# A token table in DRAM whose neighbouring places move 1152 bytes apart

## The chip, the cores and the metric

The kernel runs on one core of a Trainium2 chip. The metric is the device time of one execution in microseconds (us), lower is better. The engines named below are PE (TensorE, matrix products and transposes), DVE (VectorE), ACT (ScalarE), POOL (GpSimd) and SP (SyncE, which here only issues DMAs). All DMAs of the core, whether SP or POOL issues them, run on the same 16 DMA engines.

## The reference

Block-causal attention over 8 batches and 8 heads (576 tokens, head dimension 64, blocks of 64), then a mixture of 8 experts in which every token goes to the one expert with the largest router logit.

```
scores = q @ k.T / sqrt(64); masked to key block <= query block; softmax; out = attn @ v
x = out as (4608, 512)
logits = normalized(x) @ normalized(expert_emb).T / tau
e = argmax(logits); g = softmax(logits)[e]
out[e == i] = g * (relu(x[e == i] @ w1[i]) @ w2[i])      # w1: 512 x 1024, w2: 1024 x 512
```

## The kernel before

**Attention** works on 32 pairs of heads, four pairs to a batch. A step of the main loop computes the scores of one pair, the products with the values of the pair before, the row maxima of the next pair and the operands of the one after. The order of these parts within a step is written out by hand in strings of letters (`PLANS`): s, v, f, m, p, l for the parts of attention, and **r** for one piece of "other work", which is the router of the batch that has just ended. Each engine runs its instructions in the order in which they are written.

A row maximum goes a long way round: DVE reduces (line 338), PE transposes, ACT copies the result to `nmT` (line 345), and SP issues two small DMAs that put it as a row into `qx` (line 347). The score products of the next pair (lines 367 and 368, PE) cannot begin without it.

**The router** of a batch (`route`) finds the expert of each of the 576 tokens, its gate, and its rank within the expert. From these, `places` works out the place of the token: first place of the expert plus rank. The batch's rows of x go to DRAM (`xbuf`, lines 472 and 473), and then five indirect DMAs, issued by POOL (line 575), write 1 + token number into the place of each token in a DRAM table. Each of the five takes the 128 rows of one query tile and writes single numbers of 4 bytes, each to the address that its index gives: 576 in all, since 64 of the 640 rows stand for no token and are dropped. Seven of the eight batches do this, so 35 such DMAs run. The table has 36864 places, 36 x 128 for each of 8 experts, and place i stands at byte 4 i; ranks of an expert that follow each other are 4 bytes apart.

**The table is read twice**, both times by SP. After the seventh batch, `early_rows` reads the first 256 places (`et`, line 600), from which POOL gathers the first tokens of expert 0 (`ex`). SP takes its work in order, and the read waits for all table writes; behind it in SP's order stand the two `qx<-nmT` DMAs of the last pair. Later the whole table is read as 288 rows of 512 bytes (`tsb`, line 1014), and a product with one-hot columns (line 799) spreads the rows over the expert slots.

**The experts** follow: PE runs about 1700 products of 128 x 128 with 512 columns in split precision, nearly without a gap.

PE's sums of the softmax (lines 408 to 413) use partial sums `pS`, which POOL adds up (line 358, four additions for each head).

Of the kernel before, what the change touches and what calls it, by code (L numbers as in the profile page):

```python
# [8 lines left out]
F32 = mybir.dt.float32  # L9
F32R = mybir.dt.float32r  # L10
BF16 = mybir.dt.bfloat16
# [6 lines left out]
# of a pair of heads: the order of the parts of its scores (s), of the products with the values of  # L18
# the pair before (v) and its ends (f), of the maxima of the next pair (m), of the operands of the
# one after (p), the loads (l), and parts of the router's preparation (k) and of other work (r)  # L20
# [14 lines left out]
def kernel(  # L35
# [12 lines left out]
    nc = tc.nc  # L48
# [5 lines left out]
    NJ = (S - 64) // P + 1          # query tiles: 64 rows, then 128 each; key tiles: 128 each, then 64  # L54
    SP = NJ * P
    NTILE = B * NJ
    RW = DM + 8                     # row of x, its gate, padding
    NSLOT = NT // P + E - 1
    NFL = 5
    EARLY = 2                       # slots of the first expert that hold tokens of all batches but the last  # L60
# [7 lines left out]
    xbuf = dram.tile([NT + 1, RW], F32, name="xbuf")     # row 0: zeros; row t + 1: x of token t, its gate  # L68
    # 1 + token of each place of each expert, RE rows of places for each; 0 where empty
# [7 lines left out]
    ident = const.tile([P, P], F32, name="ident")  # L77
    make_identity(nc, ident)
    triS = const.tile([P, P], BF16, name="triS")        # triS[p, t] = p < t
# [9 lines left out]
    upto = const.tile([P, E, E], F32, name="upto")      # upto[e, f] = f <= e  # L89
# [8 lines left out]

    erev = iota("erev", [P, NJ, E], [[0, NJ], [-1, E]], E)              # E - e
    ebase = iota("ebase", [P, NJ, E], [[0, NJ], [RE * P, E]])           # first place of an expert  # L100
    tokf = iota("tokf", [P, B, NJ], [[S, B], [P, NJ]], 1 - 64, 1)       # 1 + token of row p of tile (b, j)
    gi = iota("gi", [P, NSLOT], [[1, NSLOT]])
    pio = iota("pio", [P, P], [[1, P]])
    # of each row of the table: its expert, as a one-hot, and its rank in the expert's rows
# [8 lines left out]
    drop = const.tile([P, NJ], F32, name="drop")        # large for the rows of tile 0 that stand for nothing  # L113
# [3 lines left out]
    # of each expert: its early slots; what lacks of their places is spread over the partitions  # L117
# [9 lines left out]
    acc = const.tile([P, E], F32, name="acc")           # one-hots summed over tiles  # L127
# [11 lines left out]
    CW = 1024                       # columns of a piece of the weights  # L139
# [14 lines left out]
    Q0 = 64                         # tokens stand 64 columns in, so that tile j is columns 128 j ..  # L154
    SPLIT = 5 * 64                  # queries whose sums stand in the first part
# [25 lines left out]
    NR = 6                          # tiles of q and k as they are loaded  # L181
# [11 lines left out]
    def load_v(n):  # L193
        # tiles of 128 rows, then 64
        b, h0, a = n // NP, 2 * (n % NP), vo[n % NV]
        for hh in range(2):
            nc.sync.dma_start(a[:, 0:NJ - 1, hh, :], v[b, h0 + hh, 0:S - 64, :].rearrange("(j p) d -> p j d", p=P))
        nc.sync.dma_start(a[0:64, NJ - 1, :, :], v[b, h0:h0 + 2, S - 64:S, :].rearrange("h p d -> p h d"))

    # what follows runs in the order it is written in, engine by engine  # L200
# [8 lines left out]
    # operands of the scores, split in two parts: qb = [qh; ql], qx = [qh; mask, -max],  # L209
    # ka = [kh; kh], kx = [kl; mask, ones]; scores^T = ka^T qb + kx^T qx  # L210
# [4 lines left out]
    # qh of both heads, block by block of 64, as a block diagonal; kh of both heads  # L215
    NB = S // 64
    KX = 64 + NJ + 1                # rows of qx and kx
# [34 lines left out]
    # of a pair of heads: identity, and the router's columns of each head  # L252
# [27 lines left out]
    def prep(n):  # L280
        """q and k of a pair of heads: transposed and split."""
# [46 lines left out]
    def maxes(n):  # L328
        """-max of each row of scores, into a row of qx."""
# [20 lines left out]
    # columns of P^T: key tile t holds queries 128 t .. S  # L350
# [3 lines left out]
    def add(ps, t, pT):  # L354
        """ps += key tile t of P^T; ps begins as the part of tile 0 past the first 128 queries."""
        r, w = (P if t < NJ - 1 else 64), S - P * t
        o = ps[0:r, P * (t - 1):S - P]
        nc.gpsimd.tensor_tensor(o, pT[0:r, P:S] if t == 1 else o, pT[0:r, off[t]:off[t] + w], op=ALU.add)  # L358

    def scores(n, pTs):  # L360
        """P^T = exp(scale (scores^T - max)) of a pair of heads, a key tile at a time."""
# [27 lines left out]
    def values(n, pTs):  # L389
        """out^T of a pair of heads side by side, and the sums of its rows."""  # L390
# [13 lines left out]
        # rows 0 and 32: queries up to SPLIT of either head; rows 64 and 96: the SPLIT last ones  # L404
# [15 lines left out]
    JB = 3                      # query tiles in the first of two banks  # L420

    def finish(n, xrow, rin, lgh, ssp):
        """x of a pair of heads, and its part of the router's products."""
# [9 lines left out]
        # sums of the rows of each query tile: of tile 0; of 1 and 2 and, from the same columns, 3 and 4  # L433
# [30 lines left out]
        if n >= NPAIR - NP:         # the last batch: its sums of squares pair by pair  # L464
# [17 lines left out]
    def route(b, xrow, lgh, ssp):  # L482
        """expert, gate and row of xbuf of the tokens of a batch."""
# [12 lines left out]
        # first of the largest  # L496
# [8 lines left out]
        # rank within the expert  # L505
# [24 lines left out]
        if b == B - 2:  # L530
            # the first expert's next rank: past its early slots
# [12 lines left out]
        # gate: of the scaled logits, less their largest  # L544
# [10 lines left out]
        if b < B - 1:  # L555
            rowj = yield from places(t2, ohb)
# [32 lines left out]
    def indices(eng, rows, outs, tk, none):  # L589
        """rows of xbuf and of the output of a table of tokens."""  # L590
# [6 lines left out]
    def early_rows():  # L597
        et = rt.tile([P, EARLY], F32, name="et")
        none = rt.tile([P, EARLY], F32, name="enone")
        nc.sync.dma_start(et, table[0:EARLY * P, :].rearrange("(p j) o -> p (j o)", j=EARLY))  # L600
# [15 lines left out]
    def places(t, ohb):  # L616
        """place of each token: its rank and what its expert's places start at."""
# [4 lines left out]
        nc.vector.tensor_reduce(row, t, axis=AX.X, op=ALU.add)  # L622
        yield
# [33 lines left out]
    def post(n):  # L657
        """what is left of a pair of heads after its products with the values."""
# [30 lines left out]
    # a step: a part of the scores of a pair of heads, of the values of the pair before, and of what  # L689
    # else is due: maxima of the next pair, operands of the one after, ends of the one before  # L690
# [25 lines left out]
    # weights of expert e lie, split in two, in half e % 2 of the rings; those of the next  # L716
    # expert are split in while this one's slots run, and the raw ones of the one after loaded
# [34 lines left out]
    def counts():  # L752
        """slots of each expert: those up to its last, those before its first."""
# [16 lines left out]
        # first place of an expert's table, its early slots before the others  # L770
# [3 lines left out]
    def slot_tokens():  # L774
        """rows of xbuf and of the output, of each place of each slot."""
# [445 lines left out]
```

## Time and profile before

| | us |
|---|---|
| three runs, median (lowest, highest) | 978.39 (975.14, 980.23) |
| span of the profiled execution | 972.5 |
| PE busy in it | 914.2 (94%) |
| DVE, ACT, POOL busy | 533.6, 456.4, 335.6 |

The span runs from the first to the last instruction of the program; what lies around it in an execution is not in the profile, whose own time is told by the span alone. The median of the runs is 5.9 us above the span. The attention takes the first 490 us, the experts the rest. The page's busy share is an average over both; what a change in the attention is worth has to be read from the waits there.

### The profile page before, as it was taken

The numbers are of one execution on the slowest core, as the hardware profiler recorded it, in microseconds if no ns is written. First come the engines' busy times: TensorE is split into PE (matmuls) and PEld (weight loads), VectorE is DVE, ScalarE is ACT, GpSimd is POOL, SyncE is SP. The second block draws the span as 40 slices with busy tenths as digits, with TensorE's granted clock in tenths as the row PEclk, the third lists the DMA queues.
The fourth block names the chain that finished last, engine by engine and source line by source line (L and its number), as shares of the span: only waits on it lengthen the run. The fifth ranks groups of instructions, "written<-read, shape, count | busy, mean of one in ns | idle before, by whom it ended". The sixth has DMA issues, their size and how long they took to land. (4 is left out here: it accounts for less than half of the span.)

```text
span 972.5 us, 19818 instructions
## 1 busy us (share of the span) xinstructions
PE 914.2 (94%) x5426; PEld 714.0 (73%) x5426; DVE 533.6 (55%) x1269; ACT 456.4 (47%) x923; POOL 335.6 (35%) x436
## 2 busy tenths in 40 slices
PE   5999899698998979898699999999999999999996
PEld 4677677476676757676477888888888888888885
DVE  8678677386686857777188544644343222442221
ACT  4567657275575746656366343444343222342221
POOL 5444646246364553636443111111111111111111
PEclk8899999798998999989699999999999999999999
DMA  8858679669685848767347634544444111111101
GB/s 159 174 120 165 157 147 166 93 132 151 135 183 117 168 102 161 168 138 171 115 136 239 217 132 131 188 156 132 132 131 133 45 45 46 34 47 43 44 28 54
DMA packets 155406, 122.47 MB, mean 126 GB/s; under 512 B 122233, under 2 KB 123689, under 8 KB 155260
## 3 DMA queue, kind: packets, MB, share of 16 engines
q1 hardware_dynamic: 147532, 100.14, 45.4%
q0 software_dynamic: 7728, 20.70, 6.7%
q8 instruction: 52, 0.85, 0.4%
q14 instruction: 94, 0.77, 0.3%
HBM read 72.98 MB, written 19.71 MB: 95 GB/s over the span
## 5 line engine op out<-in xcount | busy, mean ns | idle before, releaser
L377 ACT ACTIVATE pT<-pss 128x448 f32<-128x448 f32 (+1 forms) x254 | 112.8, 451 | 150.9 <-PE pss L368 112.5
L338 DVE TENSOR_REDUCE nmx<-psm 128x1 f32<-128x320 f32 x315 | 135.2, 453 | 67.7 <-PE psm L336 57.5
L961 POOL DMA_INDIRECT out_dram<-y,outi x36 | 36.1, 1002 | 356.7 <-DVE y L960 336.6
L367 PE MATMUL pss<-qb,ka 128*128 128x448 f32 (+1 forms) x382 | 130.9, 353 | 16.5 <-ACT pT L377 16.5
L358 POOL TENSOR_TENSOR pS<-pT 128x448 f32<-128x448 f32 x64 | 73.0, 1141 | 175.1 <-ACT pT L377 175.0
L368 PE MATMUL pss<-qx,kx 70*128 70x448 f32 (+1 forms) x382 | 113.5, 321 | 19.6 <-DMA qx<-nmT 19.6
L358 POOL TENSOR_TENSOR pS<-pS,pT 128x320 f32<-128x320 f32 (+2 forms) x192 | 114.1, 594 | 31.6 <-ACT pT L377 10.0
L921 PE MATMUL py<-ring_h,hh 128*128 (+1 forms) x288 | 116.4, 404 | 0.4 <-ACT hh L954 0.4
L399 PE MATMUL psb<-pT,vo 128*64 128x64 f32 (+5 forms) x768 | 114.9, 416 | 1.1 <-DVE lgh L458 1.1
L921 PE MATMUL py<-ring_h,hl 128*128 (+1 forms) x288 | 113.7, 395 | 1.7 <-DVE hl L955 1.7
L921 PE MATMUL py<-ring_l,hh 128*128 (+1 forms) x288 | 112.7, 391 | 0.0
L921 PE MATMUL ph<-ring_h,xh 128*128 x280 | 112.2, 401 | 0.0
L921 PE MATMUL ph<-ring_h,xl 128*128 x280 | 109.7, 392 | 0.0
L921 PE MATMUL ph<-ring_l,xh 128*128 x280 | 109.3, 390 | 0.0
L367 PEld LDWEIGHTS pss<-qb,ka 128*128 128x128 f32 x382 | 76.5, 200 | 38.2 <-ACT pT L377 20.0
L913 DVE TENSOR_TENSOR xl<-px,xh 128x512 fp32r<-128x512 f32 x35 | 24.2, 690 | 145.4 <-ACTq L888 119.0
L954 ACT CAST hh<-px 128x512 fp32r<-128x512 f32 x72 | 38.7, 589 | 135.1 <-PE px L952 129.8
L939 ACT ACTIVATE h<-ph 128x512 f32<-128x512 f32 x70 | 41.8, 597 | 126.0 <-ACTq L888 73.5
L336 PE MATMUL psm<-kd,qd 128*128 128x320 f32 x315 | 91.7, 355 | 3.8 <-ACT kd L316 1.9
L368 PEld LDWEIGHTS pss<-qx,kx 70*128 70x128 f32 x382 | 77.4, 203 | 21.4 <-issue 10.4
L741 DVE TENSOR_TENSOR ring_l<-raw,ring_h 128x1024 f32 (+1 forms) x64 | 77.3, 1248 | 25.4 <-ACT ring_h L737 25.3
L336 PEld LDWEIGHTS psm<-kd,qd 128*128 128x128 f32 x315 | 56.7, 200 | 41.0 <-ACT pT L384 14.6
(237 smaller groups left out, 1619.7 us busy)
## 6 DMA issues: line engine op xcount, KB each, us to landing
raw<-in_moe_w_dram SPq DMA_DIRECT2D x64, 512.0 KB
ka<-kd SPq DMA_DIRECT2D x128, 144.0 KB
qn<-in_q_dram SPq DMA_DIRECT2D x64, 144.0 KB
kn<-in_k_dram SPq DMA_DIRECT2D x64, 144.0 KB
qx<-qb SPq DMA_DIRECT2D x32, 288.0 KB
vo<-in_v_dram SPq DMA_DIRECT2D x64, 128.0 KB
xbuf<-xrow SPq DMA_DIRECT2D x7, 1040.0 KB
qx<-nmT SPq DMA_DIRECT2D x64, 2.2 KB
```

Of the source, the lines that this page charges most:

```text
L336: nc.tensor.matmul(mx[:, 0:max(e - a, 256)], qd[d][:, j, :, :], kd[d][:, a:a + max(e - a, 256)], start=True, stop=True)
L338: nc.vector.tensor_reduce(m[:, j + u:j + u + 1], mx[:, 0:e - a], axis=AX.X, op=ALU.max, negate=True)
L358: nc.gpsimd.tensor_tensor(o, pT[0:r, P:S] if t == 1 else o, pT[0:r, off[t]:off[t] + w], op=ALU.add)
L367: nc.tensor.matmul(o, ka[i][:, hh, ts], qb[i][:, hh, c0:c1], start=True, stop=False)
L368: nc.tensor.matmul(o, kx[i][0:KX, hh, ts], qx[i][0:KX, hh, c0:c1], start=False, stop=True)
L377: nc.scalar.activation(pT[:, o:o + c1 - c0], st[:, 0:c1 - c0], AF.Exp, scale=scale)
L399: nc.tensor.matmul(ob[hh * D:(hh + 1) * D, c0:c1], a[0:r, t, hh, :], pTs[hh][0][0:r, o:o + c1 - c0], start=(t == 0), stop=(c0 == 448 or t ...
L741: return eng.tensor_tensor(piece(ring_l, to, c, half), raw[i][:, c * CW:(c + 1) * CW], piece(ring_h, to, c, half).bitcast(F32), op=ALU.sub ...
L921: m = nc.tensor.matmul(out, a[:, c, :], w, start=(c == 0 and w is wh and a is sh), stop=(c == nk - 1 and a is sl_))
L939: nc.scalar.activation(h[:, f:f + 512], ph, AF.Relu)
L954: nc.scalar.copy(hh[:, f:f + 4, :], ptv)
L961: nc.gpsimd.indirect_dma_start(out=out, out_offset=bass.IndirectOffsetOnAxis(ap=to, axis=0), in_=y, in_offset=None, bounds_check=NT - 1, o ...
```

## The change

A place keeps its number, but stands elsewhere. Place i = 128 r + p, which stood at byte 4 i, now stands at entry 288 p + r, that is at byte 1152 p + 4 r. Ranks of an expert that follow each other are therefore 1152 bytes apart, except where p goes from 127 back to 0. `table_rows` takes the place of `places` for the seven batches that write the table. The readers follow: `et` takes the first two entries of each of 128 rows, and the whole table is read as 128 rows of 1152 bytes (`tbt`), transposed on PE in three pieces and copied by DVE into a tile that holds `tsb`.

```
-            rowj = yield from places(t2, ohb)
+            rowj = yield from table_rows(t2, ohb)
...
-        nc.sync.dma_start(et, table[0:EARLY * P, :].rearrange("(p j) o -> p (j o)", j=EARLY))
+        nc.sync.dma_start(et, table.rearrange("(p r) o -> p (r o)", p=P)[:, 0:EARLY])
...
+    def table_rows(t, ohb):
+        row = sm.tile([P, NJ], F32, name="row")
+        rowt = sm.tile([P, NJ], I32, name="rowt")
+        rowj = sm.tile([P, NJ], I32, name="rowj")
+        nc.vector.tensor_tensor(t, t, ohb, op=ALU.mult)
+        yield
+        nc.vector.tensor_reduce(rowj, t, axis=AX.X, op=ALU.max)
+        yield
+        nc.vector.tensor_scalar(rowt, rowj, P - 1, None, op0=ALU.bitwise_and)
+        yield
+        nc.vector.tensor_scalar(row, rowt, float(E * RE) - 1.0 / P, None, op0=ALU.mult)
+        yield
+        nc.vector.scalar_tensor_tensor(row, rowj, 1.0 / P, row, op0=ALU.mult, op1=ALU.add)
+        yield
+        nc.vector.tensor_tensor(rowj, row, drop, op=ALU.add)
+        yield
+        return rowj
...
-    tsb = st.tile([RC, NCH, P], F32, name="tsb")
-    nc.sync.dma_start(tsb, table.rearrange("(c p t) o -> p c (t o)", p=RC, t=P))
+    tbt = st.tile([P, NCH * RC], F32, name="tbt")
+    nc.sync.dma_start(tbt, table.rearrange("(p r) o -> p (r o)", p=P))
...
+    tsb = sets["xg"][0][0:RC, 0:NCH * P].rearrange("r (c t) -> r c t", t=P)
+    tps = ps_m.tile([P, 512], F32, name="psm")
+    for c in range(NCH):
+        nc.tensor.transpose(tps[0:RC, c * P:(c + 1) * P], tbt[:, c * RC:(c + 1) * RC], ident)
+    nc.vector.tensor_copy(tsb, tps[0:RC, 0:NCH * P].rearrange("r (c t) -> r c t", t=P))
     ch = chain()
```

The new function has three more pieces (`yield`) than the old one, so what follows it in `route` comes three r's later in the plan. In six of the seven batches POOL's order stays as it was. In the seventh it does not. POOL there before, from the router's power (`ss`) on; `pS` are the softmax sums and `table<-tokf,rowj` the table writes:

```order
L553 TENSOR_TENSOR ss<-ss,half 128x5
L358 TENSOR_TENSOR pS<-pS,pT 128x320
L358 TENSOR_TENSOR pS<-pS,pT 128x192
L358 TENSOR_TENSOR pS<-pS,pT 64x64
L575 DMA table<-tokf,rowj 36864x1 x5
L358 TENSOR_TENSOR pS<-pT 128x448
L358 TENSOR_TENSOR pS<-pS,pT 128x320
```

and after:

```order
L554 TENSOR_TENSOR ss<-ss,half 128x5
L359 TENSOR_TENSOR pS<-pS,pT 128x320
L359 TENSOR_TENSOR pS<-pS,pT 128x192
L359 TENSOR_TENSOR pS<-pS,pT 64x64
L576 DMA table<-tokf,rowj 36864x1 x3
L359 TENSOR_TENSOR pS<-pT 128x448
L359 TENSOR_TENSOR pS<-pS,pT 128x320
L359 TENSOR_TENSOR pS<-pS,pT 128x192
L359 TENSOR_TENSOR pS<-pS,pT 64x64
L576 DMA table<-tokf,rowj 36864x1 x2
```

Four additions now stand ahead of the last two table writes. DVE in the same batch, from the product with the one-hots (`t`, `ohb`) to the gate, before:

```order
L620 TENSOR_TENSOR t_5707<-t_5707,ohb 128x40
L622 TENSOR_REDUCE row<-t_5707 128x5
L286 TENSOR_TENSOR kx_183<-pst,kd_188 64x576
L624 TENSOR_TENSOR rowj<-row,drop 128x5
L557 TENSOR_SCALAR ss<-ss 128x5
```

and after:

```order
L634 TENSOR_TENSOR t_5731<-t_5731,ohb 128x40
L636 TENSOR_REDUCE rowj<-t_5731 128x5
L287 TENSOR_TENSOR kx_183<-pst,kd_188 64x576
L638 TENSOR_SCALAR rowt<-rowj 128x5
L640 TENSOR_SCALAR row<-rowt 128x5
L642 SCALAR_TENSOR_TENSOR row<-rowj,row 128x5
L644 TENSOR_TENSOR rowj<-row,drop 128x5
L339 TENSOR_REDUCE nmx_190<-psm 128x1
L558 TENSOR_SCALAR ss<-ss 128x5
```

Three small operations come in ahead of `rowj`, which the table writes wait for. On PE the three transposes stand between the last softmax sums and the first expert products, after:

```order
L410 MATMUL psb<-pS,ones 32x320
L414 MATMUL psb<-pS,ones 32x192 x2
L1072 MATMUL psm<-ident,tbt 96x128 x3
L941 MATMUL pss<-ring_h_6165,xh_6178 128x512
L941 MATMUL pss<-ring_l_6166,xh_6178 128x512
```

Before, the products of line 921 (now 941) followed the sums of line 413 (now 414) directly. DVE's copy of the result stands between two pieces of the weights' split and the last pair's `rin`. SP's order is the same, with `tbt` in the place of `tsb`.

## Rows read from the trace of the kernel before

**Rows 1.** Page: span; then engine, busy us, share, instructions.
```profile
span 972.5 us, 19818 instructions
PE 914.2 (94%) x5426; PEld 714.0 (73%) x5426; DVE 533.6 (55%) x1269; ACT 456.4 (47%) x923; POOL 335.6 (35%) x436
```
**Rows 2.** Windows: length; busy PE, PEld, DVE, ACT, POOL; clock; DMA; GB/s. Experts.
```profile
600.00:700.00 100.00, 100.00 (x493) 83.38 (x492) 47.72 (x64) 42.11 (x62) 16.40 (x17) 1.00 0.50 167
```
**Rows 3.** Tile table, its writes (ns min/median/max); SP's waits (us, times, longest).
```profile
L575 POOL DMA_INDIRECT table<-tokf,rowj x35: 966/972/1126, 110.2 to 456.5; - x35
...
SPq L600 <- DMA table<-tokf,rowj: 15.2, 1, 15.2
```
**Rows 4.** Timeline, seventh batch: start, us, instruction [idle before <- what ended it].
```profile
451.37 1.03 POOL L575 DMA_INDIRECT table<-tokf,rowj  x1 [0.45 <-DVE gs L565]
...
456.52 0.97 POOL L575 DMA_INDIRECT table<-tokf,rowj  x1 [0.30 <-issue]
457.50 1.15 POOL L358 TENSOR_TENSOR pS<-pT 128x448 f32<-128x448 f32 x1
458.74 1.92 POOL L358 TENSOR_TENSOR pS<-pS,pT 128x320 f32<-128x320 f32 x3
...
468.15 0.33 SPq L600 DMA_DIRECT2D et<-table  x1
468.58 1.58 SPq L347 DMA_DIRECT2D qx<-nmT  x2
...
470.47 0.61 PE L368 MATMUL pss<-qx,kx 70*128 70x288 f32 x1 [6.62 <-DMA qx<-nmT]
```
**Rows 5.** Windows, as in Rows 2, after the seventh batch's table writes.
```profile
456.00:458.00 2.00, 2.00 (x17) 1.96 (x17) 0.45 (x2) 0.17 (x1) 1.69 (x3) 1.00 0.71 34
...
464.00:466.00 2.00, 0.00 (x0) 0.00 (x0) 0.00 (x0) 0.09 (x1) 0.15 (x1) 1.00 0.00 0
```
**Rows 6.** Windows after table writes of the second and fourth batch.
```profile
168.00:170.00 2.00, 2.00 (x25) 1.60 (x24) 0.88 (x2) 0.51 (x1) 1.45 (x2) 1.00 2.60 49
...
296.40:303.20 6.80, 6.80 (x31) 6.22 (x32) 4.11 (x14) 3.98 (x9) 1.97 (x4) 0.55 0.00 0
```
**Rows 7.** Window with the last batch's rows on their way to `xbuf`, no table writes.
```profile
497.00:498.00 1.00, 1.00 (x8) 0.83 (x8) 0.96 (x2) 0.52 (x2) 1.00 (x2) 1.00 1.06 398
```
**Rows 8.** Timeline of PE: its other waits for row maxima in this part.
```profile
188.53 0.58 PE L368 MATMUL pss<-qx,kx 70*128 70x288 f32 x1 [6.38 <-DMA qx<-nmT]
...
249.04 0.37 PE L368 MATMUL pss<-qx,kx 70*128 70x288 f32 x1 [1.92 <-DMA qx<-nmT]
...
363.50 0.40 PE L368 MATMUL pss<-qx,kx 70*128 70x288 f32 x1 [3.33 <-DMA qx<-nmT]
```
**Rows 9.** Windows from the end of three such waits to the clock's return.
```profile
188.50:193.20 4.70, 4.67 (x13) 2.23 (x13) 0.57 (x1) 0.41 (x1) 0.00 (x0) 0.50 0.89 202
363.50:367.30 3.80, 3.79 (x11) 1.58 (x12) 0.00 (x0) 0.41 (x1) 0.00 (x0) 0.55 0.64 127
470.40:483.40 13.00, 12.93 (x56) 9.32 (x57) 0.65 (x4) 3.98 (x9) 6.72 (x11) 0.50 0.62 214
```
**Rows 10.** Timeline of PE: first and longest of six stops during table writes.
```profile
118.06 0.56 PE L367 MATMUL pss<-qb,ka 128*128 128x288 f32 x1 [2.73 <-ACT pT L377]
...
296.40 0.61 PE L367 MATMUL pss<-qb,ka 128*128 128x288 f32 x1 [2.93 <-ACT pT L377]
```
**Rows 11.** Window in which POOL issues three indirect reads in a row.
```profile
511.00:515.00 4.00, 4.00 (x21) 3.33 (x20) 3.16 (x16) 1.15 (x2) 2.90 (x3) 1.00 0.42 93
```
**Rows 12.** Timeline: the nearest rows to the added operations, and a wait behind them.
```profile
449.79 0.16 DVE L557 TENSOR_SCALAR ss<-ss 128x5 f32<-128x5 f32 x1
...
460.11 0.56 DVE L455 TENSOR_TENSOR xrow<-psb,rin 128x384 f32<-128x384 f32 x1
...
497.28 0.60 PE L952 MATMUL pe<-ident,h 128*128 128x128 f32 x4
...
500.94 0.18 PE L511 MATMUL psm<-ohb,triS 128*128 128x40 bf16 x1 [0.97 <-DVE ohb L503]
```

## Prediction

> **What bounds the kernel now.** I read the page's busy times first: PE is busy 94% of the 972.5 us [rows 1], and in the experts' stage, of which one window stands here, 100% at the full clock [rows 2]. What happens to the table cannot make that stage shorter. So I looked for PE's idle time in the attention, in its timeline, and took the longest gaps. They come in two kinds, and both stand right behind table writes.
>
> The first kind: PE waits for the row maxima (`qx<-nmT`), in the second, third, fifth and seventh batch, 6.38, 1.92, 3.33 and 6.62 us [rows 4, 8], 18.3 us together. In the seventh the reason is written out. POOL issues the five table writes from 451.37 to 457.49. SP's read of the table, `et`, waits 15.2 us for them, the longest wait that names the table [rows 3], and goes out at 468.15. The maxima's two DMAs stand behind it in SP's order, at 468.58, and PE goes on at 470.47 [rows 4]. So the last write, issued by 457.49, needs until 468.15, 10.7 us, to be done. The windows tell what the DMA engines do meanwhile: they are 0.71 busy at 34 GB/s, then show nothing at all while SP still waits [rows 5]. After the second batch's writes they are more than fully busy at 49 GB/s, and after the fourth's nothing moves for 6.8 us [rows 6]. In the first microseconds of that the rows for `xbuf` are on the way too; alone, the last batch's rows go through at 398 GB/s [rows 7]. So it is the single numbers of a batch, 576 in five DMAs, that hold the engines up, and with them whatever is queued on the same engines, the maxima among it. In the second, third and fifth batch SP does not wait for the table at all, and still the maxima come late.
>
> The second kind: six stops of 2.4 to 2.9 us, one in each of the first six batches, while POOL issues the table writes; ACT, DVE and PE all stand still. In the first batch POOL begins at 110.2 [rows 3] and PE goes on at 118.06 [rows 10]. The six idle times of PE add up to 16.1 us; the first and the longest stand in [rows 10].
>
> After a long gap the granted clock falls from 2.4 to 1.2 GHz for a while. Behind the first kind that is 4.67, 3.79 and 12.93 us of PE work at 0.50, 0.55 and 0.50 [rows 9].
>
> **The change, part by part.** *Writes to places 1152 bytes apart.* A tile's 128 tokens go to 8 experts, some 16 places in a row for each. Before, those 16 stand within 64 bytes of each other, and a batch fills some 290 bytes per expert, 72 numbers; so the 576 writes of one batch meet in eight small spots, and each must be put into the same few stretches of memory as its neighbours. Afterwards almost every write has a stretch of its own. The trace has no scattered 4-byte write, so the landing time is bounded from both sides: by the present 10.7 us above, or more if a distant place costs more than a near one, and by the 1.9 us from the maxima's issue at 468.58 to PE's start at 470.47 below [rows 4], a small DMA on free engines. I take about 2 us. The reason is the size of the present time: 576 numbers are 2.3 kB, and nothing that 16 engines do side by side takes that long over them; a queue at a few spots does.
>
> *Waits of the first kind.* With free engines the maxima land before they are needed in the second, third and fifth batch: 6.38 + 1.92 + 3.33 = 11.6 us. In the seventh POOL's order has changed: three writes, then four additions of 1.15 + 1.92 us, then two writes [rows 4]. At 1.29 us a write, (456.52 - 451.37) / 4, the first three end near 455.0, the additions near 458.1 and the last write near 460.7. It lands near 462.7, `et` goes out, 0.33 us, the maxima at 463.1, and PE can go on 1.9 us later, at 465.0. It was idle from 470.47 - 6.62 = 463.85. So 1.1 us of 6.62 stay, and 5.5 go. Sum: **17.1 us**. Bounds: nothing, and 18.3.
>
> *Clock.* Without the waits the clock has no reason to fall there. Half speed cost 4.67 x 0.50 + 3.79 x 0.45 + 12.93 x 0.50 = **10.5 us**. PE is busy throughout these stretches and ACT and DVE are not [rows 9], so I count all of it; the lower bound is half, if others then set the pace.
>
> *Stops of the second kind.* Between nothing and all of 16.1 us, and as much again for the half-speed stretches behind them (296.40 to 303.20 alone is 6.80 us at 0.55, 3.1 us [rows 6]). For their going: three indirect reads that POOL issues in a row stop nobody [rows 11], so indirect issues alone do not do it. Against: PE works on after them while the DMA engines still move nothing [rows 6], so the stop ends before the landing does. It follows POOL's issuing more closely than the landings, and POOL issues as before. I count **nothing** and keep the rest for the range.
>
> *Added work.* DVE: three operations more in each of seven batches, 21 at 0.16 us [rows 12], 3.4 us at most. They precede `rowj`, so POOL's first write, and with it the additions behind it, come up to half a microsecond later; PE needs those sums a step later, which hides it. If PE stood at that point, it would cost the 3.4. I take 1.0. PE: three transposes, 0.60 / 4 each, 0.45 us [rows 12], in line ahead of the experts. DVE: the copy of 96 x 384, near the 0.56 us of 128 x 384; it stands in the last batch's chain to `ohb`, for which PE already waits 0.97 us [rows 12], so all of it counts. Together **2.0 us**, bounds 0.5 and 4.4. The read as 128 rows of 1152 bytes instead of 288 of 512 is issued by 473 and needed by 490, so it costs nothing, and would only do so if it came 15 us late; `et` reads 128 pieces of 8 bytes in either kernel.
>
> *Sum.* On the span: 972.5 - 17.1 - 10.5 + 2.0 = 946.9. With the 5.9 us by which the median of the runs lies above the span: 952.8, say **953 us**.
>
> What is late next: in the seventh batch POOL's `ei` and the gather behind `et`, 5 us earlier than now, and the weights, whose loads stand behind the maxima on SP and move ahead with them.
>
> **A rule against it.** 576 numbers hold the engines up for many microseconds [rows 5, 6]. The Trainium skill (DMA: Bandwidth & Descriptors, Specifications) puts the blame on the size: a transfer under 512 bytes is done as a read-modify-write. By this rule alone the distance between places would not matter, and the landing would stay as it is; no run here yet shows which of the two it is.
>
> **The rivals.** (1) *Landing as before*: a 4-byte write costs what it costs wherever it goes. For it: nothing in the trace shows another 4-byte write to compare with. Against: the length of the hold-up. The waits stay, the engines are backed up whether the last two writes are issued early or late, and the added work comes on top: 978.4 + 2.0 = 980. 11%.
>
> (2) *The stops of the second kind go too*: 16.1 us and about ten for their clock: 953 - 26 = 927. 20%.
>
> (3) *Landing shortened by half only*: the four waits shrink to a few microseconds, and the clock still falls in the seventh batch: about 14 us won, 965. 10%.
>
> (4) *Slower by POOL's order*: where a write takes as long as before from its own issue, the last two, now behind 3.1 us of additions, send off `et`, and behind it the maxima, some 3.2 us later (460.7 instead of 457.5); PE's wait grows by that, and with all the added work at its bound it is 978.4 + 3.2 + 4.4 = 986. It decides as soon as the landing gets shorter by less than 3.2 us. 6%.
>
> (5) *Distant places cost more*: each write opens a stretch of its own. At twice the hold-up, the seventh batch's wait grows by 10.7, the second's by as much, and the others begin to wait: about 1015. 5%.
>
> That the change does not do what it says I leave out: the index, 288 p + r, is a whole number well within what the arithmetic holds.
>
> **How the numbers follow.** The forecast itself, 940 to 962, has 48%. With (2) and (3) that makes 78% faster by over 0.5% (about what a measurement of this kernel tells from no change, 973.5 to 983.3), 11% within it, 11% slower. The range leaves out (4), (5) and the lower part of (2): 925 to 984.
>
> **What would show it.** Right: SP's wait for the table falls from 15.2 us to some 10 (POOL's last issue alone is 8 us after SP begins to wait), `et` goes out within 3 us of POOL's last write, PE's gaps before line 369 (now) vanish in the second, third and fifth batch, and the clock stays up there. The windows behind table writes no longer show idle engines. Wrong: the read still goes out 10 us after the last write, or maxima still late in the second batch. If the six stops are gone as well, POOL's issuing was not their cause.

## The result, and the profile after

The changed kernel takes **945.7 us** (median of 4 runs, 944.35 to 947.26), the kernel before 976.76 us (median of 4 runs, 969.66 to 980.23). The ratio is 0.967, with a 95% interval of 0.962 to 0.972. The profiled executions differ by 27.8 us, 972.5 [rows 1] against 944.7:

```profile
span 944.7 us, 19846 instructions
PE 903.0 (96%) x5429; PEld 706.8 (75%) x5429; DVE 536.0 (57%) x1291; ACT 455.8 (48%) x923; POOL 335.5 (36%) x436
```

DVE, ACT and POOL are as busy as before; PE is busy 11 us less and idle 17 us less. Two groups of the listing by line (all scores of the attention, both halves) show where PE's idle time went. The first two rows are of before, the others of after; behind the bar stand busy us, mean ns of one, idle us ahead of them and what ended most of that:

```profile
L367 PE MATMUL pss<-qb,ka 128*128 128x448 f32 (+1 forms) x382 | 130.9, 353 | 16.5 <-ACT pT L377 16.5
L368 PE MATMUL pss<-qx,kx 70*128 70x448 f32 (+1 forms) x382 | 113.5, 321 | 19.6 <-DMA qx<-nmT 19.6
```
```profile
L368 PE MATMUL pss<-qb,ka 128*128 128x448 f32 (+1 forms) x382 | 128.1, 346 | 17.9 <-ACT pT L378 17.0 <-ACT pT L385 0.6 <-issue 0.3
L369 PE MATMUL pss<-qx,kx 70*128 70x448 f32 (+1 forms) x382 | 110.4, 313 | 2.3 <-DMA qx<-nmT 2.3
```

The waits for row maxima (`qx<-nmT`, first kind) fell from 19.6 to 2.3 us, of which 1.83 stand at the kernel's start, where there is no table yet. The stops (`<-ACT pT`, second kind) are all still there.

The writes take POOL as long as before, but SP waits 7.6 us for them instead of 15.2 [rows 3]:

```profile
L576 POOL DMA_INDIRECT table<-tokf,rowj x35: 966/971/1123, 110.6 to 443.1; - x35
```
```profile
SPq L601 <- DMA table<-tokf,rowj: 7.6, 1, 7.6
```

In the seventh batch, to be read against [rows 4], the last write's issue ends at 444.07, `et` goes out 1.2 us later instead of 10.7, and PE waits 0.45 us for the maxima instead of 6.62:

```profile
443.10 0.97 POOL L576 DMA_INDIRECT table<-tokf,rowj  x1 [0.30 <-issue]
...
445.27 0.33 SPq L601 DMA_DIRECT2D et<-table  x1
445.70 1.58 SPq L348 DMA_DIRECT2D qx<-nmT  x2
...
447.59 0.40 PE L369 MATMUL pss<-qx,kx 70*128 70x288 f32 x1 [0.45 <-DMA qx<-nmT]
```

The second batch shows the same without SP waiting for the table. Before, SP issued the maxima here, and PE could go on at 188.53 [rows 8], 10.7 us later:

```profile
177.85 1.57 SPq L347 DMA_DIRECT2D qx<-nmT  x2
```

After, PE takes up the same work 6.1 us behind the issue, and the row shows no wait:

```profile
178.94 1.56 SPq L348 DMA_DIRECT2D qx<-nmT  x2
...
185.03 0.30 PE L369 MATMUL pss<-qx,kx 70*128 70x288 f32 x1
```

The trace also records each DMA's completions. From the end of the issue of a batch's last table write to its last recorded completion, in us, batches 1 to 7 (each batch has 80 completions, one for each of five DMAs on 16 engines; of these the two traces hold 58 to 74 before and 29 to 46 after, so a true last one can be later):

```
before   9.4  17.2  13.3   7.2  12.8   6.9  10.6
after    1.9   1.5   1.6   1.3   1.5   1.5   1.2
```

### The profile page after: what moved, and what is told of

Its sections match the earlier page's. It is cut to its first block, busy times and chain, and to the rows that moved or that the text cites. A ratio compares the mean times of both kernels' runs of the same rounds, so it can differ in the third digit from the quotient of the medians.

```text
span 944.7 us, 19846 instructions
## 1 busy us (share of the span) xinstructions
PE 903.0 (96%) x5429; PEld 706.8 (75%) x5429; DVE 536.0 (57%) x1291; ACT 455.8 (48%) x923; POOL 335.5 (36%) x436
## 5 line engine op out<-in xcount | busy, mean ns | idle before, releaser
L339 DVE TENSOR_REDUCE nmx<-psm 128x1 f32<-128x320 f32 x315 | 135.1, 453 | 49.3 <-PE psm L337 38.7
L368 PE MATMUL pss<-qb,ka 128*128 128x448 f32 (+1 forms) x382 | 128.1, 346 | 17.9 <-ACT pT L378 17.0
L369 PE MATMUL pss<-qx,kx 70*128 70x448 f32 (+1 forms) x382 | 110.4, 313 | 2.3 <-DMA qx<-nmT 2.3
L400 PE MATMUL psb<-pT,vo 128*64 128x64 f32 (+5 forms) x768 | 111.3, 405 | 1.2 <-DVE lgh L459 1.2
L368 PEld LDWEIGHTS pss<-qb,ka 128*128 128x128 f32 x382 | 74.6, 195 | 39.3 <-ACT pT L378 21.2
L974 ACT CAST hh<-px 128x512 fp32r<-128x512 f32 x72 | 38.7, 589 | 134.8 <-PE px L972 134.8
L980 DVE TENSOR_SCALAR y<-py,xg 128x512 f32<-128x512 f32 x36 | 27.0, 750 | 98.9 <-PE py L941 93.4
```

The source lines that it names most:

```text
L339: nc.vector.tensor_reduce(m[:, j + u:j + u + 1], mx[:, 0:e - a], axis=AX.X, op=ALU.max, negate=True)
L368: nc.tensor.matmul(o, ka[i][:, hh, ts], qb[i][:, hh, c0:c1], start=True, stop=False)
L369: nc.tensor.matmul(o, kx[i][0:KX, hh, ts], qx[i][0:KX, hh, c0:c1], start=False, stop=True)
L400: nc.tensor.matmul(ob[hh * D:(hh + 1) * D, c0:c1], a[0:r, t, hh, :], pTs[hh][0][0:r, o:o + c1 - c0], start=(t == 0), stop=(c0 == 448 or t ...
L974: nc.scalar.copy(hh[:, f:f + 4, :], ptv)
```

## The experiments

Two things were to be told apart from the distance of the places: the order (three more steps ahead of the writes move POOL's and DVE's work, too), and the size of a write, which the change leaves alone. Then the stops.

**Order without distance.** On the kernel before, `rowj` takes as many steps as in the changed kernel; POOL, ACT and SP get its order, with places 4 bytes apart:

```diff
-            rowj = yield from places(t2, ohb)
+            rowj = yield from near_places(t2, ohb)
...
+        nc.vector.tensor_reduce(rowj, t, axis=AX.X, op=ALU.max)
+        yield
+        nc.vector.tensor_scalar(rowt, rowj, P - 1, None, op0=ALU.bitwise_and)
+        yield
+        nc.vector.tensor_scalar(row, rowt, 0.0, None, op0=ALU.mult)
+        yield
+        nc.vector.scalar_tensor_tensor(row, rowj, 1.0, row, op0=ALU.mult, op1=ALU.add)
+        yield
```

> The kernel before with three more small DVE steps ahead of rowj, so that every engine gets the order of the changed kernel, while the places stay 4 bytes apart. Theory of the places: the hold-up stays, PE waits for row maxima again in the second, third and fifth batch, 18 us in all give or take 5, the clock falls behind them, and the time is that of before or a little above, 972 to 985 us; the read of the first places goes out 7 us or more after POOL's last table write. Rival, the order: the three more steps are what moved the waits away, and the time is near that of the changed kernel, 942 to 952 us, with that read out within 3 us of the last write.

It took 992.4 us (four runs, 985.0 to 998.3), 1.020 times the kernel before (1.015 to 1.025): slower, and above the 972 to 985 us that I expected of it. Of its trace, which is of the fastest of the four runs, a group by line and two tile rows:

```profile
L368 PE MATMUL pss<-qx,kx 70*128 70x448 f32 (+1 forms) x382 | 113.7, 321 | 25.6 <-DMA qx<-nmT 25.6
```
```profile
L575 POOL DMA_INDIRECT table<-tokf,rowj x35: 966/971/1126, 110.8 to 468.8; - x35
L600 SPq DMA_DIRECT2D et<-table x1: 332/332/332, 478.7 to 478.7; - x1
```

The hold-up is there: `et` goes out 8.9 us after the last write's issue (468.8 + 0.97 to 478.7). It costs more than before, 25.6 us of waits against 19.6, because PE now waits for maxima in all seven batches: the writes come later, nearer to them. The order did not bring the gain; alone it loses 2%.

**Distance without order.** The changed kernel with its added operations in one step; POOL, ACT and SP stand in the order of the kernel before, five writes in a row in the seventh batch too:

```diff
         nc.vector.tensor_scalar(rowt, rowj, P - 1, None, op0=ALU.bitwise_and)
-        yield
         nc.vector.tensor_scalar(row, rowt, float(E * RE) - 1.0 / P, None, op0=ALU.mult)
-        yield
         nc.vector.scalar_tensor_tensor(row, rowj, 1.0 / P, row, op0=ALU.mult, op1=ALU.add)
```

> The changed kernel with its three more DVE operations issued in one step with the one before, so that POOL, PE and SP have the order of the kernel before (five table writes in a row in the seventh batch too), with places 1152 bytes apart. Theory of the places: no wait for row maxima in the second, third and fifth batch, the read of the first places goes out within 3 us of the last write, 940 to 952 us. Rival, the order: the waits come back, 968 to 980 us.

948.4 us, 0.972 of the kernel before (0.968 to 0.976). The waits are gone, the stops are not:

```profile
L369 PE MATMUL pss<-qx,kx 70*128 70x448 f32 (+1 forms) x382 | 111.0, 314 | 1.4 <-DMA qx<-nmT 1.4
L368 PE MATMUL pss<-qb,ka 128*128 128x448 f32 (+1 forms) x382 | 128.6, 348 | 17.8 <-ACT pT L378 17.6
```

So the distance is the cause, in either order. The trace is of the slowest of its five runs (952.5 us).

**How far apart.** Here the table stands in blocks of G slots, place first, slot last, so that consecutive places are 4 G bytes apart (G = 2, 4, 16); the reads at the end are rearranged to match:

```diff
-        nc.vector.tensor_scalar(row, rowt, float(E * RE) - 1.0 / P, None, op0=ALU.mult)
...
-        nc.vector.scalar_tensor_tensor(row, rowj, 1.0 / P, row, op0=ALU.mult, op1=ALU.add)
+        nc.vector.tensor_scalar(rowm, rowj, (G - 1) * P, None, op0=ALU.bitwise_and)
...
+        nc.vector.scalar_tensor_tensor(row, rowt, G - 1.0, rowj, op0=ALU.mult, op1=ALU.add)
...
+        nc.vector.scalar_tensor_tensor(row, rowm, 1.0 / P - 1.0, row, op0=ALU.mult, op1=ALU.add)
```

> The changed kernel with places 16 bytes apart: the table as blocks of four slots, the place first and the slot last in each; the read at the end takes 16-byte pieces, 9216 of them, and may come late. If writes hinder each other within 64 bytes or more, four neighbours meet in each 64 bytes and the hold-up shrinks only in part: some waits for maxima stay, and the read of the first places goes out 3 us or more after POOL's last write; 950 to 975 us. If only the same few bytes matter, or the distance counts for nothing beyond not being adjacent, it is as the changed kernel in this, 1.2 us and 942 to 952 us.

> The changed kernel with places 64 bytes apart: blocks of sixteen slots; the read at the end takes 64-byte pieces. If writes hinder each other only within one stretch of up to 64 bytes, nothing is left of the hold-up: the read of the first places goes out about 1.2 us after POOL's last write, no waits for maxima, 942 to 952 us. If the stretch is larger (some hundreds of bytes), eight or more neighbours still meet in it: the read goes out 3 us or more after the last write, with waits for maxima as in the kernel before, 955 to 980 us.

> The changed kernel with places 8 bytes apart (blocks of two slots). Theory of the 64-byte stretch: the writes that meet in one 64 bytes wait for each other, so the time from a batch's last issue to its last landing follows their number: 16 of them (4 bytes apart) took some 12 us, 4 (16 bytes apart) 3.7, 1 (64 bytes apart) 1.6; 8 of them should take 6 to 7, and waits of PE for row maxima come back in the second batch or the third, but not in all. Rival, adjacency alone: writes hinder each other only where the next number follows directly, and the landing takes 2 to 4 us as at 16 bytes. The read at the end takes 8-byte pieces, 18432 of them, and comes late by 5 to 20 us, which says nothing of either.

One run each: 945.3 us at 16 bytes and 946.2 at 64, on a chip where the kernel before took 973.9 (median of 7 runs); 970.4 at 8 bytes, on another chip, where the kernel before took 963.9 in its one run. The completions, as in the table above:

```
 8 B     8.6   8.8  10.1   8.4  10.0   8.4   9.0
16 B     3.8   2.9   3.2   3.6   4.7   3.5   1.6
64 B     1.8   1.5   2.2   1.3   1.7   1.5   1.2
```

The writes and the read of the first places in the tile rows at 8 bytes, PE's groups at 8 bytes, and the tile rows at 16:

```profile
L577 POOL DMA_INDIRECT table<-tokf,rowj x35: 966/971/1123, 110.2 to 453.3; - x35
L602 SPq DMA_DIRECT2D et<-table x1: 332/332/332, 463.3 to 463.3; - x1
```
```profile
L370 PE MATMUL pss<-qx,kx 70*128 70x448 f32 (+1 forms) x382 | 113.5, 320 | 32.9 <-DMA qx<-nmT 32.9
L369 PE MATMUL pss<-qb,ka 128*128 128x448 f32 (+1 forms) x382 | 130.0, 351 | 0.3 <-ACT pT L379 0.3
```
```profile
L577 POOL DMA_INDIRECT table<-tokf,rowj x35: 969/974/1127, 111.6 to 442.5; - x35
L602 SPq DMA_DIRECT2D et<-table x1: 332/332/332, 445.1 to 445.1; - x1
```

At 64 bytes nothing is left of the hold-up; at 16, where four of a batch's numbers share 64 bytes, it takes twice as long as with none, and no maxima come late any more; at 8, with eight in 64 bytes, it is nearly whole, and the maxima come late in all seven batches, where I had expected some. Adjacency alone, the rival of the 8-byte run, is out: the numbers at 8 bytes do not touch. My own figure there, 6 to 7 us in proportion to the neighbours, was too low as well: the growth is steep between 16 and 8 bytes. If writes hinder each other within one stretch of memory, it is longer than 16 bytes and no longer than 64; that it is a stretch is argued from these distances, not shown. The 8-byte row comes from another chip than the other two. At 8 bytes the stops are missing too (0.3 us ahead of the first score products). That cannot be put down to the distance, as the next part shows.

**The stops: POOL's time, or the writes?** The 30 writes of the first six batches are replaced by additions of zeros:

```diff
+                if b < B - 2:
+                    nc.gpsimd.tensor_tensor(zcol[:, 0:448], zcol[:, 0:448], zcol[:, 0:448], op=ALU.add)
+                    yield
+                    continue
                 w = nc.gpsimd.indirect_dma_start(
```

> The changed kernel with each of the 30 table writes of the first six batches replaced by an addition on POOL of 128 x 448, which takes about as long as a write's issue (1.15 us beside 1.27); those tokens are left out of the table, so their expert products are not made. Asks what the six stops of 2.5 to 2.8 us come from. If from POOL's time (the additions behind come late by five times 1.2 us), the stops stay. If from the indirect writes themselves, no stop of over 0.8 us is left at those places, the clock stays up behind them, and the span is 20 to 30 us below that of the changed kernel, 915 to 925 us.

Span 923.8 us, and no stop is left:

```profile
L368 PE MATMUL pss<-qb,ka 128*128 128x448 f32 (+1 forms) x382 | 126.6, 343 | 0.5 <-ACT pT L378 0.3
```

PE runs as many instructions here as in the changed kernel (5429), contrary to what I expected of the products, so the times can be compared. But the run cannot tell what the stops come from, for on its chip there was none to remove. It ran on one chip with `apart_8B`, `spread_mid` and `spread_wide`, and the seventh batch tells them from the rest. There all four issue three writes, additions and two writes, as the changed kernel does, which stops for 1.24 us. Seven other kernels with that order, on two other chips, stop for 1.19 to 1.25 us; these four do not stop there at all. `spread_mid` and `far_spread_et_late` (below) have the same instructions in the same order on PE, ACT, DVE and POOL. This is the same product in the two, `spread_mid` first:

```profile
410.34 0.40 PE L368 MATMUL pss<-qb,ka 128*128 128x288 f32 x1
```
```profile
411.70 0.40 PE L368 MATMUL pss<-qb,ka 128*128 128x288 f32 x1 [1.21 <-ACT pT L378]
```

So the missing stops of these four runs say nothing of their edits; what the stops come from has to be read from the runs on the other chips. The changed kernel itself did not run on the chip of the four; the kernel before took 963.9 us there in one run, and 969.7 or more in every run elsewhere. Whether it is the chip or something else about these runs is not known.

**Writes spread.** The changed kernel, with k free steps between the writes of the first six batches:

```diff
                 writes.append(w)
                 yield
+                for _ in range(k if b < B - 2 and j < NJ - 1 else 0):
+                    yield
```

> The changed kernel with the writes of the first six batches spread: three free steps between one and the next, so that POOL's order is three writes, addition, write, addition, write. If the stops come from writes issued in a row, they are as after the three writes of the seventh batch, 1.2 us each instead of 2.6, some 8 us less, and the span about 930 to 938 us; if each write costs its share wherever it stands, or POOL's additions are the cause, the sum of the stops stays at 15 us and the span at 940 to 950.

> As the run before with six free steps between: two writes, two additions, one write, two additions, one write, addition, one write. If writes in a row are the cause, the stops all but vanish and the clock stays up: 915 to 930 us. If each write costs its share wherever it stands, the sum stays: 940 to 950 us. If the additions, which now come in pieces, are late for PE's sums, slower than the changed kernel: 950 to 960.

> As spread_mid with two free steps: POOL issues four writes in a row, an addition, and the fifth. If a stop begins with the fourth write in a row, it is shorter than 2.6 us but over 0.8, 930 to 940 us; if only the fifth brings it on, none is left, 916 to 922.

With k = 3 it took **918.0 us**, with k = 6 922.8, both on the chip without stops, and 918.0 is below either forecast of it; with k = 2 it took 930.3 on a chip with them. On that chip k = 3 also ran, as `far_spread_et_late`. POOL's timeline in the first batch of `spread_mid`, and PE's stops in `far_spread_et_late`:

```profile
113.95 0.97 POOL L576 DMA_INDIRECT table<-tokf,rowj  x1 [0.30 <-issue]
114.95 1.15 POOL L359 TENSOR_TENSOR pS<-pT 128x448 f32<-128x448 f32 x1
116.26 0.99 POOL L576 DMA_INDIRECT table<-tokf,rowj  x1 [0.17 <-issue]
117.27 0.89 POOL L359 TENSOR_TENSOR pS<-pS,pT 128x320 f32<-128x320 f32 x1
118.33 0.99 POOL L576 DMA_INDIRECT table<-tokf,rowj  x1 [0.17 <-issue]
```
```profile
L368 PE MATMUL pss<-qb,ka 128*128 128x448 f32 (+1 forms) x382 | 126.6, 343 | 2.2 <-ACT pT L378 1.5 <-ACT pT L385 0.5
```

One addition between the third write and the fourth, and another between that and the fifth, and no stop is left in the first six batches, better than the 1.2 us each that I had allowed for; 1.21 of the 2.2 us are the seventh's. Four in a row, on the same chip, leave 1.02 to 1.44 us in each of the six, as forecast:

```profile
L368 PE MATMUL pss<-qb,ka 128*128 128x448 f32 (+1 forms) x382 | 127.1, 344 | 8.8 <-ACT pT L378 6.8 <-issue 1.5 <-ACT pT L385 0.6
```

**Additions between, order kept.** To rule out that it is the order of POOL's sums that matters, additions of zeros stand between the five writes, and POOL is away longer (on the chip of four_in_row):

```diff
+                if b < B - 2 and j < NJ - 1:
+                    nc.gpsimd.tensor_tensor(zcol[:, 0:448], zcol[:, 0:448], zcol[:, 0:448], op=ALU.add)
                 yield
```

> The changed kernel with an addition of zeros of 128 x 448 on POOL (1.15 us) between one table write and the next, in the first six batches; order and steps otherwise the same. POOL is kept from the softmax sums 4.6 us longer in each of them. If the stops come from writes issued one right behind the other, they are gone although POOL is busy longer, and the span is 917 to 930 us; if the additions behind the writes are what PE and ACT wait for, the stops grow to 5 us or more each, 955 to 980.

921.4 us, and hardly a stop (1.23 of the 2.1 us are the seventh batch's, which the edit leaves alone), though the sums behind the writes start later than in the changed kernel:

```profile
L368 PE MATMUL pss<-qb,ka 128*128 128x448 f32 (+1 forms) x382 | 126.6, 343 | 2.1 <-ACT pT L378 1.6 <-ACT pT L385 0.5
```

So POOL's time does not make the stops, and other POOL work between the writes ends them. This rests on one trace each of three kernels on one chip, `four_in_row`, `adds_between` and `far_spread_et_late`; the changed kernel, with its five in a row, was not run on it.

**Near places, spread.** The same edit with k = 3 on the kernel of the first experiment; POOL, ACT and SP in the order of spread_mid:

> The order of spread_mid on every engine, with places 4 bytes apart as in the kernel before (the kernel of near_late_order with three free steps between writes). If hold-up and stops are two separate things, the stops at the first six batches are gone and the waits for row maxima remain: 945 to 970 us, and the read of the first places goes out 7 us or more after the last write. If spreading the writes by itself cures the hold-up too, near 918 to 925.

**998.4 us**, worse than forecast:

```profile
L368 PE MATMUL pss<-qx,kx 70*128 70x448 f32 (+1 forms) x382 | 113.1, 319 | 62.5 <-DMA qx<-nmT 55.0 <-DMA vo<-in_v_dram 7.5
L367 PE MATMUL pss<-qb,ka 128*128 128x448 f32 (+1 forms) x382 | 129.1, 349 | 1.5 <-ACT pT L377 1.5
```

The stops are gone (1.5 us, of which 1.19 in the seventh batch) on a chip that has them, so they are a thing apart from the hold-up. The hold-up is as long as ever (10.9 to 15.2 us after the last write in the first six batches), but it ends later, since the writes are spread over 8 us, and the maxima meet it in full. In the fifth batch SP takes 5.60 us to issue its next two loads of `vo` and PE waits 12.09 us, while in the window no engine does anything and the DMA engines' busy share is 1.69 at 71 GB/s:

```profile
373.24 5.60 SPq L197 DMA_DIRECT2D vo<-in_v_dram  x2
...
379.94 0.61 PE L368 MATMUL pss<-qx,kx 70*128 70x288 f32 x1 [12.09 <-DMA qx<-nmT]
```
```profile
374.00:376.00 2.00, 0.00 (x0) 0.00 (x0) 0.00 (x0) 0.00 (x0) 0.00 (x0) 0.50 1.69 71
```

The kernel with the same places without spreading (near_late_order, on another chip) took 985.0 to 998.3 us, so the spreading won nothing here: what the stops cost came back as waits for the maxima, 62.5 us instead of 25.6.

**The read of the first places, later.** spread_mid still shows a wait of 1.52 us for maxima behind `et` in the seventh batch. Here `et` is issued four steps later:

```diff
-        nc.sync.dma_start(et, table.rearrange("(p r) o -> p (r o)", p=P)[:, 0:EARLY])
-        for _ in range(12):
+        for _ in range(4):
+            yield
+        nc.sync.dma_start(et, table.rearrange("(p r) o -> p (r o)", p=P)[:, 0:EARLY])
+        for _ in range(8):
             yield
```

> The kernel of spread_mid (far places, three free steps between writes) with the read of the first places issued four steps later, behind the row maxima in SP's order. In spread_mid SP waited 7.1 us for the table with the maxima behind it, and PE waited 1.52 us for them. Theory: SP's wait stands behind the maxima now, PE's wait in the seventh batch goes, and the time is 914 to 919 us, against 946 of the changed kernel and 918 of spread_mid. If instead POOL's gather behind that read now comes late for the experts, it is 919 to 923.

**918.6 us** (median of 6 runs), **0.942** of the kernel before (0.937 to 0.947). The maxima go out ahead of `et`, and no wait for the table is left on SP:

```profile
417.42 1.56 SPq L348 DMA_DIRECT2D qx<-nmT  x2
419.10 0.39 SPq L605 DMA_DIRECT2D et<-table  x1
```

What the edit itself gains is not known: spread_mid's single 918.0 comes from the chip without stops, and on this one it did not run. It is the fastest kernel with an interval. The changed kernel was not run on this chip either; by the ratios to the kernel before, 0.967 there and 0.942 here, the spreading and the later read together are worth some 24 us (an estimate), nearly as much again as the change gave.

## Why the prediction was right

Forecast 953, measured 945.7; forecast for the span 946.9, measured 944.7.

*The cause.* That 4-byte writes to neighbouring places hold up the engines, and that distance ends it, is shown: near places held up in both orders, far places in neither, and 8 and 16 bytes stand between. The estimate of 2 us for the landing came out at 1.2 to 1.9. Rivals (1), (3) and (5), which priced the landing as before, halved or longer, fall with it.

*The waits.* Forecast 17.1 us saved of 18.3; the four waits are gone but for 0.45 us in the seventh batch, where I had left 1.1. The stretch from the first table write to the last softmax sums, before and after, in one window each (columns as in [rows 2]):

```profile
110.00:490.40 380.40, 341.69 (x2431) 249.04 (x2431) 255.06 (x717) 219.02 (x506) 192.12 (x255) 0.92 0.71 144
```
```profile
110.00:462.40 352.40, 330.40 (x2434) 241.44 (x2433) 257.84 (x737) 218.65 (x506) 191.90 (x255) 0.96 0.69 155
```

PE's idle time in it fell from 38.7 to 22.0 us, by 16.7: about the 17.8 us of waits, less a stop of 1.24 us that the seventh batch now has as well.

*The clock.* The granted clock rose from 0.92 to 0.96, and PE was busy 11.3 us less for the same work and part of the three transposes; 10.5 was forecast. Where PE took up work behind the waits at 0.50 before [rows 9], in the second and the seventh batch, the clock is full after:

```profile
185.00:189.70 4.70, 4.70 (x45) 3.59 (x43) 3.68 (x9) 3.24 (x7) 1.20 (x2) 1.00 1.04 206
447.50:460.50 13.00, 11.14 (x84) 7.57 (x86) 4.97 (x12) 7.79 (x16) 9.63 (x15) 1.00 0.67 222
```

Some luck is in how near the numbers are: behind the six stops, too, PE worked less at half clock after, 26.6 us instead of 32.6 by the clock records of the two traces, which the forecast did not count. The 11.3 and the 16.7 us make the 28.0 us by which the stretch is shorter, the whole difference of the spans (27.8): next to nothing was won or lost behind it.

*The added work* was counted at 2.0 us, and only the transposes show, at 0.53 us where 0.45 was counted:

```profile
462.11 0.53 PE L1072 MATMUL psm<-ident,tbt 128*96 128x128 f32 x3
```

PE's wait for `ohb`, 0.97 us before [rows 12], which the copy should have lengthened, is 0.6 us now. This term was too high.

*The offset.* I added the 5.9 us by which the median of before lay above its span. After, the median lies 1.0 us above its own. That is 4.9 of the 7.1 us by which the forecast missed. In every execution with both numbers on record the time is 1.66 to 1.83 us above its own span (946.42 and 944.7 in the profiled one of after). So some 4.1 of the 5.9 us were the spread between executions of the kernel before, whose profiled one was faster than the median, and I carried them over as if they were fixed.

*The stops* stayed, 16.1 us then, 15.7 in the same six batches now, as counted; rival (2) did not happen. The argument for it, that the stops follow POOL's issuing and not the landings, was right as far as the landings go: the stops stayed when these became short. POOL's time, though, is not what they follow, as adds_between shows; breaking the row of writes is worth nearly as much as the change itself.

*Rival (4)*, that POOL's order makes it slower, did not happen because the hold-up went; near_late_order shows that it was a real one: with near places that order costs 2%.

*What I misread.* The 6.8 us after the fourth batch's writes in which nothing moves [rows 6] were no sign of the hold-up. The same stretch after the change looks alike, since nothing else is due there:

```profile
284.90:291.70 6.80, 6.75 (x42) 5.89 (x42) 4.49 (x15) 4.74 (x11) 2.91 (x4) 0.75 0.00 1
```

Nor does such a window show the landing itself: that batch's writes were still being completed before, until 301.9 by the table of completions (294.7 + 7.2), and in the window nothing moves.

And SP's wait for the table came out at 7.6 us, not 10: the writes began earlier against SP's own work than I had reckoned, so that the last one was issued 6.4 us after SP began to wait, not 8.

*The rule.* The Trainium skill (DMA: Bandwidth & Descriptors, Specifications) has it that a transfer under 512 bytes is done as a read-modify-write. By that alone the landing would have stayed; it fell from between 6.9 and 17.2 us to between 1.2 and 1.9, with writes of 4 bytes as before. The measurement decides: it is not the size by itself, but small writes to places near each other.

## What to carry to other kernels

A wait for one DMA can be the fault of another that shares the engines: look at what else was issued in the 10 us before. Scattered small writes should stand 64 bytes apart, at least 16, even at the cost of a transpose at the end, and where a trace shows stops as here, indirect DMAs from POOL should have other POOL work between them. What a hold-up costs depends on what is queued behind it, so an order is worth tuning again once it is gone: the same spreading made the kernel with far places some 24 us faster, by the estimate above, and won nothing with near ones. And before an edit is credited with an effect, look whether the effect's object was there to begin with on that chip: four runs here show no stops because their chip had none, and a place that their edits left alone gave it away.

## What was not expected of the hardware

- 576 numbers of 4 bytes take 7 to 17 us to land after the last issue when 16 share 64 bytes, 8.4 to 10.1 when 8 do, 1.6 to 4.7 when 4 do, 1.2 to 2.2 when none does. The time on the engine that issues them is the same, 0.97 us each.
- Five such writes issued in a row stop PE, ACT and DVE for mostly 2.4 to 2.9 us, on the chips that show stops. In the changed kernel's first batch the last sums on which DVE's copy rests start at 114.33 and take 0.34 us, and both DVE and ACT go on only at 118.1, with no releaser that the trace could name:

```profile
114.33 0.34 PE L414 MATMUL psb<-pS,ones 128*32 128x192 f32 x2
...
118.08 0.49 DVE L416 COPY su<-psb 97x320 f32<-97x320 f32 x1 [3.50 <-remote]
118.12 0.44 ACT L378 ACTIVATE pT<-pss 128x320 f32<-128x320 f32 x1 [3.91 <-remote]
...
118.61 0.61 PE L368 MATMUL pss<-qb,ka 128*128 128x288 f32 x1 [2.83 <-ACT pT L378]
```

So it looks as if PE's signals came late, not its work. What holds them is open. With POOL work between the writes there is next to no stop; and in the four runs of one chip there is none either way, at 8 bytes even with five writes in a row. A row of writes is not enough for a stop, then. The traces of those four runs differ in one thing more: they hold 73 to 80 of the 80 completions of a batch, mostly all, and no batch in the others has more than 77. Whether the recording has a part in the stops is open too.
